# Induced attention and a squared-ReLU FFN on one core: a batch's product with w_in in four column strips, spread to all rows by way of DRAM

## The chip, the cores and the metric

The kernel runs on one core of a Trainium2 chip. A core has five engines, each with an instruction stream of its own and in order: TensorE (PE, with its weight loads shown as PEld), VectorE (DVE), ScalarE (ACT), GpSimd (POOL) and SyncE (SP), which here issues nearly all DMAs. The metric is the device time of one execution in microseconds: lower is better. Before the change it is 1634.57 us, the median of three runs (1631.74 to 1636.58).

## What is computed

Four batches of 12480 rows of 128 numbers go through two attentions and then an FFN. In the first attention 32 inducing rows ask and the batch's rows answer, which gives a small matrix h (32 x 128) for each batch; in the second the batch's rows ask and h answers. All of it is fp32.

```
def mab(q, kv):
    s = scale * (q @ kv.transpose(0, 2, 1))
    s = s - s.max(-1, keepdims=True)
    a = np.exp(s)
    a /= a.sum(-1, keepdims=True) + 1e-09
    return a @ kv
h = mab(I, x)              # I: 32 inducing rows; h: 32 x 128 a batch
out = mab(x, h)            # 12480 x 128 a batch
...
g = np.maximum(out @ w_in, 0.0)     # w_in: 128 x 2048
return g * g @ w_out                # w_out: 2048 x 128
```

## The kernel before, in words

**Tiles and stages.** A batch is cut into 13 units of 960 rows, 52 units in all, and a unit into two FFN blocks of 480 columns. `First` (L384) handles the first attention of a unit: load, transpose (by PE for the first batch, by VectorE's 32 x 32 transposes later), scores in four strips of 32 columns (L457), softmax parts, and a product that adds to h. `first_end` (L561) closes a batch: it joins the four partial h and brings them to SBUF as hT, which has 128 columns: each of the 32 rows of h stands there four times. `Second` (L651) makes the second attention's weights of a unit: scores in strips (L661, tile na), softmax by VectorE and ScalarE, a split into a high and a low part (tile sw, L707 and L710), and a trip through DRAM (tile far, L716) that brings the weights back as st, on all 128 rows (L721). `ffn_block` (L780) does the FFN.

**The product hw.** The second attention's a @ h and the FFN's product with w_in are joined: h @ w_in is made once per batch and the attention weights st are multiplied with it. In `first_end`, `wide(k)` (L619) multiplies hT with 512 of the 2048 columns of w_in for k = 0 to 3, into a PSUM bank of its own. All 128 rows come out, each row of h @ w_in four times. `part(k)` (L623, ScalarE) copies the 128 x 512 result, rounded to fp32r, into hw k; `rest(k)` (L627, VectorE) puts the remainder, the result less its rounded copy, into rows 64 to 127. So rows 0 to 63 hold the high parts and the others the low ones, and one fp32r product over 128 rows with st (whose rows hold high and low parts in turn) gives a nearly full fp32 product. There is one buffer for each hw k, so a new one can be written when the last readers of the old one, the h matmuls of quad k in the last block of the batch before, are done.

**The FFN block.** For each of the four quads j: four h matmuls (L802) with hw j and st, two relus (L810, ScalarE), one square (L820, ScalarE), the rounding to hi (L827 on VectorE, or a casting DMA issued by POOL, L825), the remainder lo (L831, VectorE), and twelve op matmuls (L847: hi with wo_hi, hi with wo_lo, lo with wo_hi). The h matmuls of a block run ahead of its op matmuls. A block ends with a transpose (L863) and four stores (L867).

**Weights.** At the start w_in and w_out, which arrive as pairs of 32-bit words, are turned into fp32 and, for w_out, split, by chains of VectorE, ScalarE and POOL steps (L280 to L309, L351, L368 to L373).

**The order of the work.** Every step is a task in a `Plan` (L45): an engine, a cost in ns, a due time, what it needs, which buffers it takes and reads. `Plan.run` (L81) is a list scheduler: on each engine it takes, of the tasks that could start now, the one with the earliest due time, and the order that comes out is the order of the program on each engine. A task of DMA has an issue time on SP, and lands later by 900 ns, its `moves` and 1000 ns (L149 to L151); buffers named in `IN_TURN` (L55), sw and xq among them, are taken in the order in which the tasks were added; a task that needs an SP task, and is on SP itself, may follow it directly in the plan (L93), and waits for the landing on the chip. The main loop (L902) runs over units with a `PERIOD` of 31000 ns; `PERIOD / 2` is a block. Before the change the four wides of a batch are due at 5/8 to 8/8 of the last unit of the batch before; in the start all four are due from `t_end + 2000` (L883) and the first scores of `Second` at `t_end + 2000` too (L886).

Of the kernel before, what the change touches and what calls it, by code (L numbers as in the profile page):

```python
# [11 lines left out]
F32 = mybir.dt.float32  # L12
F32R = mybir.dt.float32r
# [7 lines left out]
P = 128  # L21
TS = 120
NT = 8
UNIT = TS * NT
# [20 lines left out]
class Plan:  # L45
# [17 lines left out]
    def add(self, engine, ns, fn, due, needs=(), port=False, mode=None, takes=(), reads=(), late=None, moves=0.0, lag=0.0):  # L63

        if late is None:
            late = self.LATE["PE" if engine == "PE" else "other"] if due > self.begin else 0.0  # L70
        needs = [n for n in needs if n is not None]
        t = Task(engine.split("|"), ns, fn, due, needs, port, mode, takes, late, len(self.tasks), moves, lag)
        for b in list(takes) + list(reads):
            b.users.append(t)
        for b in takes:
            if b.tag in self.IN_TURN:
                b.turn = self.turns[b.tag] = self.turns.get(b.tag, -1) + 1
        self.tasks.append(t)
        return t
# [86 lines left out]
def induced_attention_then_squared_relu_ffn(  # L166
# [8 lines left out]
    nc = tc.nc  # L175
    B, N, C = x.shape
    M = inducing.shape[0]
    F = w_in.shape[1]
# [5 lines left out]
    NQ = NF // 4  # L184
    LANE, WIDE = UNIT // Q, 256
# [3 lines left out]
    PERIOD, START, T_MAIN, NARROW, STEP = 31000.0, 2500.0, 56000.0, -6000.0, 1700.0  # L189
    W_DUE = [12000.0 + 7500.0 * k for k in range(4)] + [40000.0 + 4000.0 * k for k in range(4)]  # L190
    W_AHEAD = 9000.0
    LAG, CAST_LAG, TWICE = 1500.0, 1500.0, (4, 8)

    ST = "ACT|DVE"
# [5 lines left out]
    xq_pool = ctx.enter_context(tc.tile_pool(name="xq", bufs=2))  # L200
    xt_pool = ctx.enter_context(tc.tile_pool(name="xt", bufs=NU + 2))
    hw_pool = ctx.enter_context(tc.tile_pool(name="hw", bufs=1))
    att = ctx.enter_context(tc.tile_pool(name="att", bufs=2))
    tiny = ctx.enter_context(tc.tile_pool(name="tiny", bufs=3))
    ps_h = ctx.enter_context(tc.tile_pool(name="ps_h", bufs=2, space=PSUM))
    ps_o = ctx.enter_context(tc.tile_pool(name="ps_o", bufs=2, space=PSUM))
    ps_m = ctx.enter_context(tc.tile_pool(name="ps_m", bufs=2, space=PSUM))
    far = ctx.enter_context(tc.tile_pool(name="far", bufs=2, space=bass.MemoryType.DRAM))
    plan = Plan(dict(xn=3, early=EB, xt=NU + 2, m=2, h=2, o=2, g=GB, hi=HB, lo=LB, st=2, sw=1, rows=1, xq=2, hw0=1, hw1=1, hw2=1, hw3=1, words=3, set=2), T_MAIN)

    def bank(name):
        return ps_m.tile([P, 512], F32, tag="m", name=name)
# [33 lines left out]
    add = plan.add  # L246
# [311 lines left out]
        t = add("PE", 520, mix, due, [f.et_done], mode="n", takes=[bank_h], reads=[f.bx])  # L558
        f.add_up(t, lambda: v["hp"], bank_h, due)

    def first_end(b, due, step, wide_due, wide_step):  # L561

        v = {}
        s = state[b]
# [44 lines left out]
            s["hT"] = att.tile([C, P], F32, tag="hT", name=f"hT_{b}")  # L609
            copy(tj, s["hT"], v["hp"][:C, :P])  # L610

        def wide(k):
            if b:
                v["wp", k] = bank(f"wp_{b}_{k}")
            elif k < 2:
                v["wp", k] = ps_h.tile([P, 2, 512], F32, tag="h", name=f"wp_{b}_{k}")[:, 0, :]
            else:
                v["wp", k] = ps_o.tile([P, 512], F32, tag="o", name=f"wp_{b}_{k}")
            nc.tensor.matmul(v["wp", k], s["hT"], w_in_sb[:, k * 512:(k + 1) * 512], start=True, stop=True)  # L619

        def part(k):
            s["hw", k] = hw_pool.tile([P, 512], F32R, tag=f"hw{k}", name=f"hw_{b}_{k}")
            nc.scalar.copy(s["hw", k], v["wp", k])  # L623

        def rest(k):
            lo = slice(2 * M, 4 * M)
            nc.vector.tensor_sub(s["hw", k][lo], v["wp", k][lo, :], s["hw", k][lo])  # L627

        bl, bz, bj = Buffer("m"), Buffer("m"), Buffer("m")
        t = add("DVE", 70, lanes, due, [last.shifted])  # L630
# [7 lines left out]
        t = add("DVE", 200, spread, due, [t])  # L638
        t = add("PE", 140, join, due + step, [t, last.summed], takes=[bj])
        tj = s["joined"] = add("ACT|DVE", (200, 200), joined, due + step, [t], reads=[bj])  # L640
        s["wide"] = []
        for k in range(F // 512):
            bw = Buffer("m" if b else "h" if k < 2 else "o")
            s["bhw", k] = Buffer(f"hw{k}")
            d = wide_due + k * wide_step
            t = add("PE", 870, lambda k=k: wide(k), d, [s["joined"], w_ins[k]], takes=[bw, s["bhw", k]])
            p = add("ACT", 650, lambda k=k: part(k), d, [t], reads=[bw, s["bhw", k]])
            s["wide"].append(add("DVE", 725, lambda k=k: rest(k), d, [p], reads=[bw, s["bhw", k]]))


    class Second:  # L651
# [228 lines left out]
        firsts[u] = First(0, u, 6000 + START * u, early=True)  # L880
        first_alone(firsts[u], 6000 + START * u)
    t_end = 6000 + START * NU + 2000
    first_end(0, t_end, 1000, t_end + 2000, 1000)  # L883
    t_main = T_MAIN
    seconds = {0: Second(0, 0)}
    narrow(seconds[0], None, None, t_end + 2000, 800)  # L886
    seconds[1] = Second(0, 1)
    narrow(seconds[1], None, None, t_end + 10000, 1700, seconds[0].split)
    opened = [add("POOL", 1, open_g, t_main - 2000, [firsts[NU - 1].summed])]
# [12 lines left out]
    for w, (b, u) in enumerate(units):  # L902
        t_u = t_main + w * PERIOD
        for k in range(2):
            ffn_block(b, u, k, seconds[w], t_u + k * PERIOD / 2, [] if w else opened)
        if w + 1 == len(units):
            break
        nxt = units[w + 1]
        if nxt[1] == 0:
            first_end(nxt[0], t_u - PERIOD / 2, 2000, t_u + PERIOD * 5 / 8, PERIOD / 8)  # L910
        before = seconds[w - 1].ready[1] if w else None
        if w:
            seconds[w + 1] = Second(*nxt)
        for m in range(1 + (w in TWICE)):
            g = firsts[done] if state.get("last") is not firsts[done] else None
            f = next_first(t_u + NARROW, seconds[0].ready[0])
            narrow(None if m or not w else seconds[w + 1], f, g, t_u + NARROW, STEP, before)
# [33 lines left out]
```

## Time and profile before

| | |
|---|---|
| median of 3 runs | 1634.57 us (1631.74 to 1636.58) |
| the profiled execution | 1636.69 us, span 1634.9 us, mean granted clock of TensorE 0.989 |
| PE busy | 1596.4 us |
| ScalarE busy | 1542.2 us |
| VectorE busy | 1461.1 us |
| wp matmuls (L619) | 32 instructions, two for each of the 16 products |
| hw copies (L623) and subtractions (L627) | 16 each |
| first FFN matmul h | at 77.38 us of the span |
| DMA | 311.00 MB, mean 190 GB/s |

The span runs from the first to the last instruction of the core. Busy time counts overlapping instructions of an engine once. An fp32 matmul appears as two instructions, an fp32r one as one; matmuls are pipelined, so that the distance between starts says more than the durations, which overlap. A row of the timeline gives start, busy time, engine, line, operation, output and inputs, count, and in brackets the idle time of the engine before it and what ended it. SPq rows are DMA issues by SP: the time is that of the issue, not of the transfer.

### The profile page before, as it was taken

What the parts mean: (1) busy time and instruction counts of PE and PEld (TensorE: products, weight loads), DVE (VectorE), ACT (ScalarE), POOL (GpSimd) and SP (SyncE); (2) the same over time, 40 slices, a digit from 0 to 9 for tenths busy, and PEclk for the clock granted to TensorE, in tenths of its full rate; (3) what the DMA queues carried; (4) which work ended last, traced back from release to release, by engine and by line L of the source; (5) the groups of instructions that cost most, each with busy time, mean ns of one, the idle gap of its engine ahead of it and who ended that gap; (6) DMA issues with size and microseconds to landing.
All of it is one profiled execution on the core that took longest, in us unless ns stands there. A gap on an engine that the chain in (4) does not pass through costs nothing.

```text
span 1634.9 us, 23534 instructions
## 1 busy us (share of the span) xinstructions
PE 1596.4 (98%) x8689; PEld 1325.2 (81%) x8689; DVE 1461.1 (89%) x1598; ACT 1542.2 (94%) x1566; POOL 124.0 (8%) x218
## 2 busy tenths in 40 slices
PE   7499999999999999999999999999999999999998
PEld 4278788888888888888887888888888888888887
DVE  5799989988999989999889999999888998989897
ACT  6399999999999999999998999999999999999996
POOL 1300000000000000000000000000000000000000
PEclk9699999999999999999999999999999999999999
DMA  9389988888777888788878878766555655565653
GB/s 230 71 123 202 217 217 199 212 211 210 188 207 199 209 211 203 211 207 210 217 182 202 209 207 203 211 190 190 164 181 160 190 184 172 181 199 169 192 172 95
DMA packets 474014, 311.00 MB, mean 190 GB/s; under 512 B 365212, under 2 KB 444668, under 8 KB 473900
## 3 DMA queue, kind: packets, MB, share of 16 engines
q1 hardware_dynamic: 445100, 112.89, 38.9%
q0 software_dynamic: 28800, 196.62, 33.9%
q8 instruction: 68, 1.11, 0.3%
q14 instruction: 46, 0.38, 0.1%
HBM read 74.50 MB, written 38.34 MB: 69 GB/s over the span
## 4 chain that ended last, share of the span: by engine, by line
PE 90%; DMA 3%; ACT 3%; DVE 2%; issue 1%; SPq 1%; DVEq 0%; ACTq 0%
PE op L847 63%; PE h L802 21%; PE na L661 2%; DMA xn<-in_x_dram 1%; ACT g L810 1%; ACT g L820 1%; PE wp L619 1%; PE na L457 1%; PE nb L508 1%; DVE lo L831 1%; DMA xq<-in_x_dram 1%; PE xtp L439 1%; PE ep L488 1%; DMA far<-sw 0%; PE sp L457 0%
## 5 line engine op out<-in xcount | busy, mean ns | idle before, releaser
L831 DVE TENSOR_TENSOR lo<-g,hi 128x1920 fp32r<-128x1920 f32 x416 | 883.6, 2145 | 28.5 <-PE op L847 23.1
L810 ACT ACTIVATE g<-h 128x960 f32<-128x960 f32 x832 | 781.2, 987 | 37.2 <-PE h L802 30.4
L820 ACT ACTIVATE g<-g 128x1920 f32<-128x1920 f32 x416 | 760.9, 1829 | 4.4
L802 PE MATMUL h<-st,hw 128*128 128x480 f32 x1664 | 504.6, 387 | 16.7 <-DMA st<-far 15.8
L847 PE MATMUL op<-hi,wo_lo 128*128 128x480 f32 x1664 | 472.0, 381 | 0.0
L847 PE MATMUL op<-hi,wo_hi 128*128 128x480 f32 x1664 | 442.3, 381 | 0.0
L847 PE MATMUL op<-lo,wo_hi 128*128 128x480 f32 x1664 | 435.0, 381 | 2.6 <-DVE lo L831 2.6
L802 PEld LDWEIGHTS h<-st,hw 128*128 128x128 f32 x1664 | 306.1, 189 | 78.6 <-DVE sw L710 15.8
L847 PEld LDWEIGHTS op<-lo,wo_hi 128*128 128x128 f32 x1664 | 309.9, 188 | 54.5 <-DVE lo L831 5.8
L847 PEld LDWEIGHTS op<-hi,wo_lo 128*128 128x128 f32 x1664 | 312.1, 188 | 50.9 <-issue 2.1
L847 PEld LDWEIGHTS op<-hi,wo_hi 128*128 128x128 f32 x1664 | 310.9, 188 | 49.8 <-issue 1.6
L827 DVE CAST hi<-g 128x1920 fp32r<-128x1920 f32 x216 | 248.4, 1152 | 37.5 <-PE op L847 26.6
L825 POOL DMA_DIRECT2D hi<-g x200 | 107.0, 535 | 1424.9 <-ACT g L810 279.3
L863 DVE STREAM_TRANSPOSE rows<-op 128x480 f32<-128x480 f32 x104 | 70.4, 677 | 51.2 <-PE op L847 49.5
L424 DVE STREAM_TRANSPOSE xt<-xq 128x960 f32<-128x960 f32 x39 | 45.6, 1170 | 8.6 <-DMA xq<-in_x_dram 6.0
L661 PEld LDWEIGHTS na<-xt,hT 128*32 128x32 f32 x520 | 19.9, 110 | 25.2 <-issue 19.4
L661 PE MATMUL na<-xt,hT 128*32 128x256 f32 (+2 forms) x520 | 34.9, 351 | 0.0
L685 ACT ACTIVATE d<-d 128x256 f32<-128x256 f32 x52 | 22.8, 439 | 7.0 <-DVE d L682 7.0
L689 DVE TENSOR_REDUCE z<-d 128x8 f32<-128x256 f32 x52 | 20.7, 398 | 8.4 <-ACT d L685 8.4
L508 PE MATMUL nb<-xn,et 120*32 120x128 f32 x624 | 25.7, 275 | 0.0
L457 PE MATMUL na<-xt,indT 128*32 128x240 f32 x312 | 24.8, 373 | 0.0
L703 DVE STREAM_TRANSPOSE a<-d 128x256 f32<-128x256 f32 x52 | 23.0, 443 | 1.3
(86 smaller groups left out, 529.6 us busy)
## 6 DMA issues: line engine op xcount, KB each, us to landing
hi<-g POOLq DMA_DIRECT2D x200, 960.0 KB, 4.5
xn<-in_x_dram SPq DMA_DIRECT2D x52, 480.0 KB, 6.3
st<-far SPq DMA_DIRECT2D x104, 240.0 KB, 4.3
out_dram<-rows SPq DMA_DIRECT2D x416, 60.0 KB, 3.5
xq<-in_x_dram SPq DMA_DIRECT2D x156, 120.0 KB, 5.3
far<-sw SPq DMA_DIRECT2D x52, 240.0 KB, 2.5
words_i<-in_moe_w_in_dram SPq DMA_DIRECT2D x4, 512.0 KB, 15.8
words_o<-in_moe_w_out_dram SPq DMA_DIRECT2D x4, 512.0 KB, 7.1
```

Of the source, the lines that this page charges most:

```text
L424: nc.vector.transpose(self.xt, v["xq"].rearrange("p g c -> p (g c)"))
L457: nc.tensor.matmul(to, indT, from_, start=True, stop=True)
L508: nc.tensor.matmul(where[q * M:(q + 1) * M, :], self.et[:, k, q * M:(q + 1) * M], self.xn[:, 2 * q + k, :], start=(k == 0), stop=(k == 1),)
L661: nc.tensor.matmul(where[q * M:(q + 1) * M, to:to + n], self.s["hT"][:, :2 * M].rearrange("c (m a) -> c m a", a=2)[:, :, 0], self.s["xt"][ ...
L802: nc.tensor.matmul(c["hp"][:, l, :BLK], s["hw", j][:, f % 4 * P:(f % 4 + 1) * P], s["st", u][:, k, :], start=True, stop=True,)
L810: nc.scalar.activation(v["g"][:, 2 * i:2 * i + 2, :], c["hp"][:, :, :BLK], AF.Relu)
L820: nc.scalar.activation(v["g"], v["g"], AF.Square)
L825: nc.gpsimd.dma_start(v["hi"], v["g"])
L827: nc.vector.tensor_copy(v["hi"], v["g"])
L831: nc.vector.tensor_sub(v["lo"], v["g"], v["hi"])
L847: nc.tensor.matmul(w["op"][:, :BLK], wo[:, 4 * j + l, :], v[name][:, l, :], start=len(done) == 1, stop=len(done) == 3 * NF,)
L863: nc.vector.transpose(w["rows"].rearrange("p g c -> p (g c)"), w["op"][:, :BLK])
```

## The change

`wide` becomes one task per batch: it multiplies the 32 distinct columns of hT (every second of the first 64) with each of the four parts of w_in, into the four strips of 32 rows of one PSUM bank. So the bank holds the 32 rows of h @ w_in once, 512 columns in each strip. `part(i)` and `rest(i)` then split the bank in two pieces of 256 columns, into a tile with a high and a low half: in the main loop this is the sw buffer that `Second` uses too (one buffer), in the start a room of the xq pool. `away(i)` sends the piece to DRAM, and `back_in(k)` brings strip k back to hw k with four DMAs of 32 rows of 512 numbers each, the high part to rows 0 to 63 (even rows and odd rows), the low part to rows 64 to 127. All copies wait for both aways. ScalarE and VectorE then work on 256 columns twice, where they had 512 columns four times. All of w_in has to be ready for the one task; before, each part of it alone.

The due times change as well: in the main loop the product is due 4000 ns before the last unit of the batch before begins, and the copies back from that unit's middle on, an eighth of the period apart. In the start the first scores of `Second` are due at `t_end + 500`, ahead of the product, which stays at `t_end + 2000`; the copies back are due from `t_end + 3000` on, 1000 apart.

```diff
+    WIDE_AT, BACK_AT = -4000.0, 0.0
...
-        def wide(k):
+        def wide():
+            v["wp"] = bank(f"wp_{b}")
+            thin = s["hT"][:, :2 * M].rearrange("c (m a) -> c m a", a=2)[:, :, 0]
+            for k in range(NQ):
+                nc.tensor.matmul(
+                    v["wp"][k * M:(k + 1) * M, :], thin, w_in_sb[:, k * 512:(k + 1) * 512], start=True, stop=True
+                )
+
+        def part(i):
             if b:
-                v["wp", k] = bank(f"wp_{b}_{k}")
-            elif k < 2:
-                v["wp", k] = ps_h.tile([P, 2, 512], F32, tag="h", name=f"wp_{b}_{k}")[:, 0, :]
+                v["hw", i] = att.tile([P, 2, WIDE], F32R, tag="sw", name=f"hwp_{b}_{i}", bufs=1)
             else:
-                v["wp", k] = ps_o.tile([P, 512], F32, tag="o", name=f"wp_{b}_{k}")
-            nc.tensor.matmul(v["wp", k], s["hT"], w_in_sb[:, k * 512:(k + 1) * 512], start=True, stop=True)
-
-        def part(k):
+                room = xq_pool.tile([P, UNIT // M, M], F32, tag="xq", name=f"hwp_{b}_{i}")
+                v["hw", i] = room.rearrange("p g c -> p (g c)")[:, :2 * WIDE].rearrange("p (j n) -> p j n", j=2).bitcast(F32R)
+            nc.scalar.copy(v["hw", i][:, 0, :], v["wp"][:, i * WIDE:(i + 1) * WIDE])
+
+        def rest(i):
+            nc.vector.tensor_sub(v["hw", i][:, 1, :], v["wp"][:, i * WIDE:(i + 1) * WIDE], v["hw", i][:, 0, :])
+
+        def away(i):
+            if i == 0:
+                v["far"] = far.tile([P, 2, 512], F32, tag="hwfar", name=f"hwfar_{b}", bufs=1)
+            nc.sync.dma_start(v["far"][:, :, i * WIDE:(i + 1) * WIDE], v["hw", i].bitcast(F32))
+
+        def back_in(k):
             s["hw", k] = hw_pool.tile([P, 512], F32R, tag=f"hw{k}", name=f"hw_{b}_{k}")
-            nc.scalar.copy(s["hw", k], v["wp", k])
-
-        def rest(k):
-            lo = slice(2 * M, 4 * M)
-            nc.vector.tensor_sub(s["hw", k][lo], v["wp", k][lo, :], s["hw", k][lo])
+            rows = s["hw", k].rearrange("(r a) n -> a r n", a=2).bitcast(F32)
+            for a in range(2):
+                for j in range(2):
+                    nc.sync.dma_start(rows[a, j * M:(j + 1) * M], v["far"][k * M:(k + 1) * M, j, :])
...
+        bw = Buffer("m")
+        t = add("PE", 950, wide, wide_due, [s["joined"]] + w_ins, takes=[bw])
+        far_done = []
+        for i in range(2):
+            bp = Buffer("sw" if b else "xq")
+            p = add("ACT", 420, lambda i=i: part(i), wide_due + 500, [t], takes=[bp], reads=[bw])
+            p = add("DVE", 400, lambda i=i: rest(i), wide_due + 1000, [p], reads=[bp, bw])
+            far_done.append(add("SP", 600, lambda i=i: away(i), wide_due + 2000, [p], reads=[bp], moves=1000))
         s["wide"] = []
-        for k in range(F // 512):
-            bw = Buffer("m" if b else "h" if k < 2 else "o")
-            s["bhw", k] = Buffer(f"hw{k}")
-            d = wide_due + k * wide_step
-            t = add("PE", 870, lambda k=k: wide(k), d, [s["joined"], w_ins[k]], takes=[bw, s["bhw", k]])
-            p = add("ACT", 650, lambda k=k: part(k), d, [t], reads=[bw, s["bhw", k]])
-            s["wide"].append(add("DVE", 725, lambda k=k: rest(k), d, [p], reads=[bw, s["bhw", k]]))
+        for k in range(NQ):
+            bh = s["bhw", k] = Buffer(f"hw{k}")
+            s["wide"].append(add("SP", 2400, lambda k=k: back_in(k), back_due + k * back_step, far_done, takes=[bh], moves=1000,
+                                 lag=LAG if b else 0.0))
...
-    first_end(0, t_end, 1000, t_end + 2000, 1000)
+    first_end(0, t_end, 1000, t_end + 2000, t_end + 3000, 1000)
...
-    narrow(seconds[0], None, None, t_end + 2000, 800)
+    narrow(seconds[0], None, None, t_end + 500, 800)
...
-            first_end(nxt[0], t_u - PERIOD / 2, 2000, t_u + PERIOD * 5 / 8, PERIOD / 8)
+            first_end(nxt[0], t_u - PERIOD / 2, 2000, t_u + WIDE_AT, t_u + PERIOD / 2 + BACK_AT, PERIOD / 8)
```

More of the change, by code (lines that the diff above doesn't have):

```diff
@@ L559, in mix_alone, with first_end @@
         f.add_up(t, lambda: v["hp"], bank_h, due)
-    def first_end(b, due, step, wide_due, wide_step):
+    def first_end(b, due, step, wide_due, back_due, back_step):
         v = {}
```

## The prediction

> **What bounds the kernel now.** I read the page first: busy times, then the chain that ended last.
>
> ```profile
> PE 1596.4 (98%) x8689; PEld 1325.2 (81%) x8689; DVE 1461.1 (89%) x1598; ACT 1542.2 (94%) x1566; POOL 124.0 (8%) x218
> ```
>
> ```profile
> PE 90%; DMA 3%; ACT 3%; DVE 2%; issue 1%; SPq 1%; DVEq 0%; ACTq 0%
> ```
>
> TensorE carries the chain, but ScalarE is close behind it. Averages hide stages, so I read the waits of PE next, and then the windows of one unit's length (29.9 us; columns: PE, PEld, DVE, ACT and POOL busy, granted clock, DMA share, GB/s).
>
> ```profile
> PE h L802 <- DMA st<-far: 15.8, 1, 15.8
> ```
>
> ```profile
> 436.20:466.10 29.90, 29.90 (x140) 24.17 (x142) 26.46 (x31) 29.50 (x32) 2.11 (x4) 1.00 0.78 180
> ```
>
> So there are two places. Once, before the first FFN block, PE stands still for 15.8 us until st arrives. After that it is busy without a gap: 29.90 of 29.90 us in the window that holds three of batch 1's four wp products. There, each us of work taken off PE is a us of the span as long as nothing else ends later, and the one to watch is ScalarE with 29.50 of 29.90.
>
> **Part 1: the products, in the three batch ends of the main loop.** The timeline of PE shows both a product as it is now and a score in strips (L661), which has the form that the change gives to the product.
>
> ```profile
> 462.21 1.02 PE L619 MATMUL wp<-w_in_sb,hT 128*128 128x512 f32 x2
> 462.67 0.99 PE L802 MATMUL h<-st,hw 128*128 128x480 f32 x2
> 463.50 0.60 PE L847 MATMUL op<-hi,wo_lo 128*128 128x480 f32 x2
> 463.93 1.02 PE L847 MATMUL op<-lo,wo_hi 128*128 128x480 f32 x4
> 464.79 0.60 PE L802 MATMUL h<-st,hw 128*128 128x480 f32 x2
> 465.23 0.60 PE L847 MATMUL op<-hi,wo_hi 128*128 128x480 f32 x2
> 465.76 0.63 PE L661 MATMUL na<-xt,hT 128*32 128x256 f32 x9
> 466.22 0.38 PE L457 MATMUL na<-xt,indT 128*32 128x240 f32 x3
> ...
> 467.21 0.71 PE L847 MATMUL op<-hi,wo_hi 128*128 128x480 f32 x2
> 467.76 0.60 PE L847 MATMUL op<-hi,wo_lo 128*128 128x480 f32 x2
> ```
>
> Ends are modelled, so I use starts. From 462.21 to 463.50 PE does one product wp (two instructions) and two h; 1.29 us. Two FFN matmuls take 0.43 (the pair at 463.50 is followed at 463.93). So one product takes 0.86, and the four of a batch 3.44 us.
>
> The scores of a second unit are strips side by side: from 465.76 to 466.22 four strips of up to 256 columns and a stub of 16 pass in 0.46 us. One after another, at the rate of wp (0.86 for 512 columns), they would have taken 4 x 0.43 = 1.72. So strips do overlap here. For 512 columns I double it: 0.92. Around such a group there is a price for going over to strips and back: 465.23 plus 0.43 is 465.66, so 0.10 goes before the group, and the pair after it takes 0.55 (467.21 to 467.76) where 0.43 is normal, 0.12 more. Product in strips: 0.92 + 0.22 = 1.14. PE saves 3.44 - 1.14 = 2.30 per batch, 6.9 us over three batches. Ends for this term: without the price of going over, 2.52 x 3 = 7.6; if strips overlapped in pairs only (2 x 0.86 + 0.22 = 1.94), 1.50 x 3 = 4.5. I take 6.9, since the row that shows strips is this kernel's own.
>
> The Trainium skill, "TensorE: Matmul & The Clock Gate", section "Measured speedup vs the span model", gives 2.38x for three column strips of 512. By that rate four products would cost an estimated 3.44 / 2.38 = 1.45 us of strips and the term would be 3 x (3.44 - 1.67) = 5.3; the 0.46 us above speaks for nearly full overlap, and the sum stays with the row.
>
> **Part 2: the split, in the loop.** What is removed and what takes its place:
>
> ```profile
> L623 ACT CAST hw<-wp x16: 567/586/597, 56.4 to 1249.9; 128x512 fp32r<-128x512 f32 x16
> ```
>
> ```profile
> L627 DVE TENSOR_TENSOR hw<-wp,hw x16: 694/695/696, 57.0 to 1253.3; 64x512 fp32r<-64x512 f32 x16
> ```
>
> ```profile
> L250 ACT COPY et<-ep 120x256 f32<-120x256 f32 x3 | 1.2, 388 | 0.0
> ```
>
> ```profile
> L675 DVE STREAM_TRANSPOSE d<-na 128x256 f32<-128x256 f32 x3 | 1.3, 436 | 0.0
> ```
>
> ScalarE gives up 4 x 0.586 = 2.34 and gets two copies of 256 columns from PSUM, 2 x 0.388 (L250's row) = 0.78: 1.57 less per batch. VectorE gives up 4 x 0.695 = 2.78 and gets two of 0.436 (L675's row): 1.91 less. Both lie beside PE and are counted at nothing. If PE were not the bound there, ScalarE's 1.57 would be the gain (a rival below).
>
> The split now holds one psum bank for both parts, and the second part reuses the one sw buffer. So part(1), on ScalarE, waits until the first away has landed. Behind it on ScalarE stand the relus and squares; for the relus PE waits, which has only two h banks.
>
> ```profile
> L716 SPq DMA_DIRECT2D far<-sw x52: 552/552/1260, 70.0 to 1573.0; - x52
> ```
>
> ```profile
> DMA to landing us min/median/max: 2.5/2.5/7.4
> ```
>
> The kernel's plan knows this wait: it allows about 0.6 + 0.9 + 1.0 + 1.0 and 0.2 of margin, 3.7 us from the away's start, and lets other ScalarE work go first. A transfer of this size lands in 2.5 at the median, 7.4 at most. So the wait costs from 0 to 3.7 us per batch; I take 0, as the median is the nearest value.
>
> **Part 3: the copies, in the loop.** SP gets 18 more issues per batch: two aways, and sixteen copies back of 64 KB each.
>
> ```profile
> L867 SPq DMA_DIRECT2D out_dram<-rows x416: 315/497/2941, 104.6 to 1631.9; - x139
> ```
>
> ```profile
> L420 SPq DMA_DIRECT2D xq<-in_x_dram x156: 322/672/3862, 73.9 to 1072.5; - x156
> ```
>
> ```profile
> st<-far SPq DMA_DIRECT2D x104, 240.0 KB, 4.3
> ```
>
> ```profile
> 455.69 3.35 SPq L867 DMA_DIRECT2D out_dram<-rows  x4
> 467.36 0.34 SPq L400 DMA_DIRECT2D xn<-in_x_dram  x1
> 468.57 8.26 SPq L420 DMA_DIRECT2D xq<-in_x_dram  x4
> ```
>
> The nearest row is the store, 60 KB over 32 rows in runs of four: 0.497 each. Sixteen take 8.0 us, four of them 2.0. hw of quad k is free when its last reader in the last block is done and is needed one block, 15 us (half of 29.9), later. Four issues and a landing (4.3, as st's) are 6.3 us: 8.7 to spare, so it costs nothing. Each copy waits at the head of SP for PE's readers; stores, loads and st queue behind it. SP has a gap of 8.3 us here (459.04 to 467.36), and no engine needs those transfers at once. Were this cover gone, each us by which hw is late would be one of PE.
>
> **Part 4: the start.** Here the change moves the order: the first scores now come ahead of the product on PE, and the copies of hw come ahead of st on SP.
>
> ```profile
> 53.91 0.27 ACT L250 COPY hT<-htp 128x128 f32<-128x128 f32 x1 [3.79 <-PE htp L606]
> ```
>
> ```profile
> 54.32 2.05 PE L619 MATMUL wp<-w_in_sb,hT 128*128 128x512 f32 x2 [0.45 <-ACT hT L250]
> 56.30 1.11 PE L661 MATMUL na<-xt,hT 128*32 128x256 f32 x10
> ...
> 77.38 1.14 PE L802 MATMUL h<-st,hw 128*128 128x480 f32 x2 [15.76 <-DMA st<-far]
> ```
>
> ```profile
> 58.23 0.42 DVE L679 TENSOR_REDUCE mx<-d 128x8 f32<-128x256 f32 x1
> ...
> 61.68 0.69 DVE L627 TENSOR_TENSOR hw<-wp,hw 64x512 fp32r<-64x512 f32 x1 [0.16 <-ACT hw L623]
> 62.41 0.43 DVE L682 TENSOR_TENSOR d<-d,mx 128x256 f32<-128x256 f32 x1
> ```
>
> ```profile
> 70.04 0.64 SPq L716 DMA_DIRECT2D far<-sw  x1
> 72.59 1.27 SPq L721 DMA_DIRECT2D st<-far  x2
> ```
>
> ```profile
> 54.30:61.70 7.40, 7.30 (x28) 2.84 (x28) 2.97 (x6) 3.38 (x6) 2.53 (x2) 0.68 0.01 2
> ```
>
> Two paths then meet at st. The softmax path: na starts at 54.3 instead of 56.30, 2.0 earlier. Now, 3.8 us pass between the maximum (ends 58.65) and the subtraction (62.41), with three rests in them; the change leaves two short ones, and I credit 2.5 of the 3.8. So sw is ready at 70.04 - 4.5 = 65.5.
>
> The hw path: na is done at 55.4; the strips take what one product takes there, 2.05 (the granted clock in this stretch was 0.68), so 57.5; copy 0.39, subtraction 0.44, the second pair beside them, two aways of 0.55 each: the second starts at about 59.3 and lands 2.5 later, with 0.2 of handing over at 62.0. By the due times in the code SP then issues the copies of hw0 to hw2 (12 x 0.497 = 6.0, to 68.0), st's away (0.64, to 68.6), the copies of hw3 (2.0, to 70.6), and only then st. st's away has landed by 70.5, so st is issued at 70.6, where it was 72.59: 2.0 earlier, and first h with it at 75.4. PE stays idle for it all the same; what is late next is SP's queue, no longer the softmax. Ends: at 0.32 a copy (the least in both rows) hw2 is out at 65.8, st's away lands at 68.3, the gain is 4.3; at 0.672 (the median of xq) st goes at 73.4, a loss of 0.8. I take 0.497, the row nearest in size and rows. The loads of x behind st move with it.
>
> **The sum.** The profiled execution took 1636.69 us (span 1634.9): less 6.9 and 2.0 is 1627.8. It lies 2.1 above the median of the runs, 1634.57; against that the forecast is 1634.57 - 8.9 = 1625.7.
>
> **Rivals.** *The copies go one at a time.* For: the four xq at 468.57 take 8.26 us, 2.07 each. Against: their median is 0.672, the stores' 0.497. At 2.07 the sixteen and st's away would take 33.8 us from 62.0, st would leave at 95.8 and the first h come 23 us late: 1634.6 - 6.9 + 23.2 = 1651, slower. It decides from where the start loses more than the loop's 6.9: st at 79.5, so (79.5 - 62.0 - 0.64) / 16 = 1.05 us a copy. The Trainium skill, "DMA: Bandwidth & Descriptors", section "Rules for kernel authors", says that transfers to disjoint partitions serialize and that one of 128 partitions should be used; with its fit of 2.0 us plus bytes an estimated 16 x 2.15 = 34 us would pass, the same end. The medians above are against it. Chance 0.08.
>
> *ScalarE waits for the first part's landing* (part 2). For: a landing of 7.4 has been seen, and ScalarE has 0.4 us to spare in the window. Against: median 2.5, and the plan's allowance of 3.7. At 2 us a batch it takes 6 back, 1631.7, which is within 0.3%; at the full 3.7 it is 1636.8, still within. Chance 0.12.
>
> *ScalarE is the bound at the batch ends.* Then a batch gains 1.57, not 2.30: 4.7 + 2.0, 1627.9. For: 29.50 of 29.90. Against: PE shows no gap there. Chance 0.20.
>
> *The strips don't overlap*, so that the change doesn't do what it says: 4 x 0.86 + 0.22 costs 0.2 more per batch and the start's gain goes with the later product: about 1635. The strips of L661 speak against it. Chance 0.03.
>
> **How the numbers follow.** The forecast has 0.55; 0.02 is left for what I don't see. A measurement of this kernel can tell about 0.3%, 4.9 us, from no change. Faster by more than that (below 1629.7) are the forecast and ScalarE as bound, 0.75, less 0.01 for their edges: 0.74. Within it are the waiting ScalarE, the strips and the rest: 0.17. Slower: 0.09, nearly all from the copies. The range takes the ends of the two terms (7.6 + 4.3 gives 1622.7, 4.5 less 0.8 gives 1630.9), 1.7 below for the spread of runs, and above reaches into the case of the waiting ScalarE: 1621 to 1633.
>
> **What would show it.** In the profile after: wp (now strips) with a spacing of some 1.1 us between its neighbours in the loop; the first h at about 75.4, st issued after the last copy of hw; copies on SP at about 0.5 apiece in the start; PE still 29.9 of 29.9 in the batch ends. Wrong if PE waits for hw or st at a batch end, if ScalarE shows an idle stretch before the second part, or if the copies are over 1 us apart.

## The result, and the profile after

The changed kernel takes 1650.97 us at the median of six runs, the kernel before 1634.68 in the same comparison: a ratio of 1.0097, with a 95% interval from 1.0083 to 1.0112. That is 16 us slower, where 9 us faster was forecast. One of the six executions took 2125.95 us at a granted clock of 0.689; the comparison leaves it out, and the profile read here is of another execution of the changed kernel, of 1648.56 us (span 1646.8, mean granted clock 0.984), beside which the kernel before took 1634.24.

The busy times and the chain that ended last, on the page of the changed kernel:

```profile
PE 1591.8 (97%) x8689; PEld 1323.9 (80%) x8689; DVE 1450.1 (88%) x1590; ACT 1534.8 (93%) x1558; POOL 123.5 (8%) x218
```

```profile
PE 90%; DVE 3%; DMA 3%; ACT 2%; SPq 1%; issue 1%; DVEq 0%; ACTq 0%; POOLq 0%
```

These two lines tell almost nothing: PE is busy 4.6 us less, ScalarE and VectorE are relieved as meant, and the chain looks as it did. What is new stands in the waits of PE:

```profile
PE h L822 <- DMA st<-far: 19.4, 1, 19.4
PE h L822 <- DMA hw<-hwfar: 12.1, 3, 6.2
```

By its name the new wait is for hw; which transfer each of these rests hung on is read further down. The windows of the three batch ends (columns as in the prediction: length, PE, PEld, DVE, ACT, POOL, granted clock, DMA share, GB/s):

```profile
436.20:466.10 29.90, 28.80 (x158) 23.48 (x157) 26.96 (x29) 28.71 (x30) 2.11 (x4) 1.00 0.80 206
466.10:496.00 29.90, 22.90 (x123) 18.51 (x122) 17.39 (x22) 19.34 (x21) 1.58 (x3) 0.89 0.92 210
854.80:884.70 29.90, 24.82 (x138) 20.32 (x128) 20.75 (x29) 19.49 (x22) 1.59 (x3) 0.89 0.88 194
1243.50:1273.40 29.90, 27.86 (x122) 23.61 (x121) 24.63 (x24) 25.84 (x23) 2.11 (x4) 0.94 0.73 208
```

The second and the third of them in the kernel before (the prediction shows the first; the last is as full, 29.90):

```profile
466.10:496.00 29.90, 29.90 (x192) 24.64 (x185) 28.16 (x33) 28.59 (x30) 1.59 (x3) 1.00 0.85 209
854.80:884.70 29.90, 29.36 (x188) 23.52 (x187) 26.96 (x32) 25.19 (x28) 1.59 (x3) 1.00 0.81 190
```

PE stands still for 1.10 + 7.00 + 5.08 + 2.04 = 15.2 us in these four windows, where it stood for 0.5 before. And the three windows with a long rest in them were granted 0.89, 0.89 and 0.94 of the clock. If all of their busy time ran at that mean, it would have cost (22.90 + 24.82) x 0.11 + 27.86 x 0.06 = 6.9 us, an estimate. The stretches with the lower clock give the same: from 481.3 to 488.1, from 870.4 to 877.2 and from 1259.5 to 1262.9 us it was granted at 0.50, and PE was busy for 4.53, 5.80 and 3.40 us of them, half of which is 6.9. So 14.7 more of idle time, some 6.9 of slow clock, less the 6.9 forecast for the strips: some 14.7, against 11.9 between the two profiled spans, 14.3 between the two executions of that comparison and 16 between the medians.

The Trainium skill, "TensorE: Matmul & The Clock Gate", section "HAM oscillation — how this bites in real kernels", says that PE-idle gaps over about 3.4 us throttle the clock again. The gaps of 6.2 and 5.08 us agree with it; the longest recorded gap of the last window is 2.0 us and it fell to 0.94 all the same, for which that rule has no reason.

Who held hw back is seen on SP, at the end of batch 1 (start, time of issue, line, tiles, count):

```profile
450.10 2.41 SPq L642 DMA_DIRECT2D hw<-hwfar  x4
452.61 4.07 SPq L887 DMA_DIRECT2D out_dram<-rows  x4
456.77 0.56 SPq L736 DMA_DIRECT2D far<-sw  x1
459.94 1.28 SPq L741 DMA_DIRECT2D st<-far  x2
461.31 6.93 SPq L642 DMA_DIRECT2D hw<-hwfar  x8
468.29 0.59 SPq L401 DMA_DIRECT2D xn<-in_x_dram  x1
468.97 5.49 SPq L421 DMA_DIRECT2D xq<-in_x_dram  x4
474.56 5.81 SPq L642 DMA_DIRECT2D hw<-hwfar  x4
```

```profile
476.32 1.03 PE L867 MATMUL op<-lo,wo_hi 128*128 128x480 f32 x4
483.57 1.94 PE L822 MATMUL h<-st,hw 128*128 128x480 f32 x4 [6.22 <-DMA hw<-hwfar]
```

The rest of SP of 8.3 us, on which the prediction leaned, is gone: from 450.10 to 480.37 SP has no gap of note but one, of 2.6 us, in which st waits at its head for far to land. The sixteen copies take 2.41 + 6.93 + 5.81 = 15.15 us of it, 0.95 each. The copy of hw 3 stands last: st, eight other copies and five loads of x go first. It lands at about 483.4 and PE, whose FFN is out of work at 477.35, has waited for 6.2 us. Before that, at 468.88, PE had waited 0.78 us for the copies of hw 1.

Batch 2 shows a second way in which the change delays PE. Here is the end of VectorE's split into sw, the first weights of the new batch, before and after:

```profile
838.61 0.43 DVE L710 TENSOR_TENSOR sw<-a,sw 128x256 fp32r<-128x256 f32 x1
```

```profile
854.22 0.42 DVE L730 TENSOR_TENSOR sw<-a,sw 128x256 fp32r<-128x256 f32 x1
```

The split ends 15.6 us later. Its buffer is the one in which part(0) and then part(1) of hw lay, each until its away had landed (the two aways were issued from 839.58 to 847.58). Then SP comes on top: stores and four copies are ahead of far, which goes at 858.78, and st leaves at 863.85. PE's rest of 5.08 us ends at 871.40 with the first four h of the new batch, which need hw 0 and st. The view names hw as what it waited for, but that hw 0 had been sent from 849.57 on, and st was the late one, by its time from issue to landing:

```profile
L741 SPq DMA_DIRECT2D st<-far x2: 613/713/813, 863.8 to 864.5; - x2
DMA to landing us min/median/max: 6.3/6.5/6.7
```

The second of the two, issued at 864.5, took the 6.7 and landed at 871.3, just ahead of PE's start. The rest of 2.04 us at the end of batch 3 is of the same kind: the view names a square of ScalarE, but the second half of st, issued at 1251.4, landed after 6.8 us at 1258.2, and PE went on at 1258.32. A rest of 0.63 us, at batch 1's end, ended like this too, at 465.03, with st landed at 464.9. Of the 15.2 us, then, 7.0 are waits for hw, all at batch 1's end, and 7.75 are waits for st, at all three.

### The profile page after: what moved, and what is told of

It is laid out like the page before. It is cut to its first block, busy times and chain, and to the rows that moved or that the text cites. A ratio compares the mean times of both kernels' runs of the same rounds, so it can differ in the third digit from the quotient of the medians.

```text
span 2124.2 us, 23623 instructions
## 1 busy us (share of the span) xinstructions
PE 2089.6 (98%) x8689; PEld 1437.5 (68%) x8689; DVE 1467.2 (69%) x1590; ACT 1578.7 (74%) x1558; POOL 122.6 (6%) x218
## 4 chain that ended last, share of the span: by engine, by line
PE 98%; DVE 1%; DMA 0%; ACT 0%; SPq 0%; issue 0%; ACTq 0%
PE op L867 68%; PE h L822 23%; PE na L681 2%; PE nb L509 1%; PE na L458 1%; PE ep L489 1%; PE xtp L440 1%; PE hp L509 0%; PE sp L458 0%; DMA xn<-in_x_dram 0%; PE wp L617 0%; DMA xq<-in_x_dram 0%; ACT g L830 0%; SPq L642 0%; DVE a_o L300 0%
## 5 line engine op out<-in xcount | busy, mean ns | idle before, releaser
L822 PE MATMUL h<-st,hw 128*128 128x480 f32 x1664 | 627.5, 469 | 20.4 <-DMA st<-far 19.5
L867 PE MATMUL op<-hi,wo_lo 128*128 128x480 f32 x1664 | 603.0, 467 | 0.0
L867 PE MATMUL op<-hi,wo_hi 128*128 128x480 f32 x1664 | 575.7, 468 | 0.0
L867 PE MATMUL op<-lo,wo_hi 128*128 128x480 f32 x1664 | 561.2, 468 | 0.0
L822 PEld LDWEIGHTS h<-st,hw 128*128 128x128 f32 x1664 | 338.0, 205 | 165.3 <-issue 40.2
L867 PEld LDWEIGHTS op<-hi,wo_lo 128*128 128x128 f32 x1664 | 339.1, 204 | 140.4 <-issue 17.2
L867 PEld LDWEIGHTS op<-lo,wo_hi 128*128 128x128 f32 x1664 | 336.4, 203 | 140.4 <-issue 19.1
L867 PEld LDWEIGHTS op<-hi,wo_hi 128*128 128x128 f32 x1664 | 336.5, 203 | 139.8 <-issue 19.6
L251 ACT COPY et<-ep 120x256 f32<-120x256 f32 x52 | 19.3, 372 | 38.0 <-PE ep L489 38.0
L509 PEld LDWEIGHTS nb<-xn,et 120*32 120x32 f32 x624 | 20.6, 114 | 13.8 <-issue 8.8
```

Of the source, the lines that this page charges most:

```text
L509: nc.tensor.matmul(where[q * M:(q + 1) * M, :], self.et[:, k, q * M:(q + 1) * M], self.xn[:, 2 * q + k, :], start=(k == 0), stop=(k == 1),)
L822: nc.tensor.matmul(c["hp"][:, l, :BLK], s["hw", j][:, f % 4 * P:(f % 4 + 1) * P], s["st", u][:, k, :], start=True, stop=True,)
L867: nc.tensor.matmul(w["op"][:, :BLK], wo[:, 4 * j + l, :], v[name][:, l, :], start=len(done) == 1, stop=len(done) == 3 * NF,)
```

## The experiments

**Theory 1**: SP issues in order, and with 18 more issues at each batch end it is full, so that hw, or st behind hw, comes late. **Theory 2**: the two parts hold the sw buffer through two landings, so the new batch's first sw, and with it st, comes late. **Theory 3**: not the number of issues but the bytes, 1 MB back in per batch, slow the transfers down. In the diffs, lines are those of the changed kernel.

**a0_after.** The changed kernel without an edit, for a profile.

> The changed kernel itself, unaltered, for an undisturbed trace. First theory: the 16 us that it lost lie at the three batch ends of the main loop, since the first h started at the same time as before; then PE shows idle stretches there of some 5 us each, ended by the landing of a copy of hw (theory 1) or by ScalarE, which stood waiting for the first part's landing (theory 2). Rival: the loss is spread over all units (theory 3), by DMA traffic or by another order of the steps, and then no stretch of PE stands out. About 1650 us in all three cases.

It took 1648.56 us, and its profile is the one read above.

**e1_nocopy.** No copies in the loop:

```diff
+            if b:
+                s["wide"].append(add("POOL", 1, lambda k=k: s.update({("hw", k): state[0]["hw", k]}), back_due + k * back_step, far_done))
+                continue
```

> The product in strips, its split and the aways stay, but in the three batch ends of the main loop nothing is copied back (batches 1 to 3 use the hw of batch 0, so that part of the result is left out). Theory 1 (SP's queue, in order, is the bound at a batch end: what hangs on it, hw or st, comes late): without the sixteen issues the waits of PE go, and what is left is the saving of the strips, 1634.7 less 6.9, so 1627 to 1629. Theory 2 (the parts hold the sw buffer and the PSUM bank, so the first st of the new batch is late): those waits stay, some 7 of the 13 us that PE now stands still or runs slow at the second and third batch end, 1637 or more. Theory 3 (the traffic of the copies): like theory 1.

1635.24 us, ratio 1.0009 (0.9989 to 1.0028): the copies cost 16 us, the whole loss. But the saving didn't appear either. The profiled execution, at 1647.13 the slowest of ten and the only one with a trace, shows why that can be:

```profile
PE h L826 <- DMA st<-far: 28.9, 3, 19.5
```

Twice, for 9.4 us in all, PE waited for st at a batch end, with no copy in the queue. That speaks for theory 2.

**e2_pool_queue.** The loop's copies are issued by POOL:

```diff
-                    nc.sync.dma_start(rows[a, j * M:(j + 1) * M], v["far"][k * M:(k + 1) * M, j, :])
+                    (nc.gpsimd if b else nc.sync).dma_start(rows[a, j * M:(j + 1) * M], v["far"][k * M:(k + 1) * M, j, :])
```

> All copies stay, those of the main loop are issued by POOL instead of SP; POOL issues only the casts there. Theory 1: SP is free of them, 1627 to 1632. Theory 2: no gain at the second and third batch end, 1637 or more. Theory 3 (the same bytes on the same DMA engines): no gain at all, 1648 to 1651.

1646.83 us (1639.33 to 1650.69), ratio 1.0065 (1.0040 to 1.0089). No wait for hw is left, but another took its place:

```profile
PE h L822 <- DMA st<-far: 23.7, 2, 19.5
PE op L867 <- DVE lo L851: 10.9, 7, 8.2
```

The 4.2 us that the first line has beyond the start's 19.5 are at batch 2's end, as theory 2 has it. The longest wait for lo, 8.2 us, ends at 527.30, over 60 us after POOL issued the last copy of that batch end (462.56 to 464.58). VectorE, which makes lo, stood in front of it for the rows buffer of the block before:

```profile
524.52 0.68 DVE L883 STREAM_TRANSPOSE rows<-op 128x480 f32<-128x480 f32 x1 [7.71 <-DMA out_dram<-rows]
```

The stores of that block left SP only from 517.37 to 521.71, behind loads of x (6.32 us for four), far (3.43 us for one issue) and st. So with the copies on another engine it is still the queue of SP that runs late; what made its issues slow there was not tried apart. The Trainium skill, "DMA: Bandwidth & Descriptors", section "Rules for kernel authors", says that spreading DMAs over the issuing engines only saves the sequencer's issue time; the gain over the changed kernel, 4 us between medians whose intervals overlap, agrees.

**e3_half_issues.** Scratch DRAM holds each piece twice, row beside row, so that a copy back fills 64 rows:

```diff
-            nc.sync.dma_start(v["far"][:, :, i * WIDE:(i + 1) * WIDE], v["hw", i].bitcast(F32))
+            for a in range(2):
+                nc.sync.dma_start(
+                    v["far"][:, :, a, i * WIDE:(i + 1) * WIDE].rearrange("j p n -> p j n"), v["hw", i].bitcast(F32)
+                )
...
-            for a in range(2):
-                for j in range(2):
-                    nc.sync.dma_start(rows[a, j * M:(j + 1) * M], v["far"][k * M:(k + 1) * M, j, :])
+            for j in range(2):
+                nc.sync.dma_start(
+                    s["hw", k][2 * j * M:2 * (j + 1) * M].bitcast(F32), v["far"][j, k * M:(k + 1) * M].rearrange("m a n -> (m a) n")
+                )
```

> The parts go to DRAM twice, row by row, and come back in two copies of 64 rows for each hw instead of four of 32: per batch 4 aways and 8 copies instead of 2 and 16, the bytes back as before, the bytes away doubled. Theory 1: SP is relieved of 6 of 18 issues, some 4 us per batch end, of the 5 to 8 us by which hw or st is late: 1633 to 1642. Theory 2: unchanged or worse, 1650. Theory 3: more bytes, so worse, 1650 or more.

1641.85 us, ratio 1.0033 (1.0012 to 1.0054): 9 us better with twelve issues in place of 18, the same bytes back and twice the bytes away. By the names of the view the wait for hw hardly fell (11.2 us, from 12.1). By the landings the gain is st's: of the 7.75 us for which PE waited for st at the batch ends 1.3 are left, while the waits for hw grew from 7.0 to 9.9. The rest in the start went from 19.4 to 16.2. Theory 3 alone would have had no gain.

**e4_own_buffer and e5_own_buffer_nocopy.** The parts get a buffer of their own; room for it comes from a single tile d in `Second` and from hT, which keeps 64 columns. The second kernel has no copies either, as e1.

```diff
-                v["hw", i] = att.tile([P, 2, WIDE], F32R, tag="sw", name=f"hwp_{b}_{i}", bufs=1)
+                v["hw", i] = att.tile([P, 2, WIDE], F32R, tag="hwp", name=f"hwp_{b}_{i}", bufs=1)
...
-            bp = Buffer("sw" if b else "xq")
+            bp = Buffer("hwp" if b else "xq")
...
-                v["d"] = tile_of("d")
+                v["d"] = tile_of("d", 1)
```

> The changed kernel, but the parts of hw get a buffer of their own instead of the sw buffer of the second attention (room for it: one tile d instead of two, and hT with its 64 used columns alone). After the run without the copies, which came out at 1635, two causes are held: theory 1, SP's queue with the sixteen copies (about 16 us of the loss), and theory 2, the sw buffer, which the first unit of a new batch gets only after two transfers have landed, so that its st is late (about 7 us, what was missing there from 1628). Theory 2 alone right: 1634 or less for this kernel. Both: 1640 to 1645, as the copies stay. Theory 1 alone: 1649 to 1651, as now.

> The own buffer, and no copies back in the main loop (batches 1 to 3 use the hw of batch 0: that part of the result is left out). Theories 1 and 2 together: no wait is left at the batch ends and only the saving of the strips stands, 1627 to 1629. If it stays at 1633 to 1636, as with the sw buffer, theory 2 falls and the saving on PE was mis-sized.

1653.16 us (ratio 1.0111, 1.0096 to 1.0126) and 1634.87 (0.9997, 0.9988 to 1.0007). Read by themselves these times say that theory 2 is worth nothing. The windows say otherwise. Here are two of e5, the second at batch 1's end:

```profile
137.00:197.00 60.00, 52.20 (x296) 42.11 (x289) 50.35 (x65) 49.85 (x56) 3.80 (x7) 0.94 1.05 211
466.10:496.00 29.90, 29.90 (x153) 25.37 (x144) 27.18 (x30) 29.09 (x30) 2.11 (x4) 1.00 0.80 212
```

The batch end is full, but far from any batch end PE now stands for 7.8 of 60 us, where the kernel before stood for 1.9 (58.12 busy): the single d moved the order of the work there. The edit had a side effect as large as what it was to measure, so both kernels were made anew, as e8 and e9.

**e6_own_half_issues and e7_own_half_loads.** e4 with e3's halved issues; and that with the x loads of a batch's second unit put behind the last copy of hw:

```diff
-            f = next_first(t_u + NARROW, seconds[0].ready[0])
+            f = next_first(t_u + NARROW, state[b]["wide"][-1] if b and not u else seconds[0].ready[0])
```

> The own buffer, and twelve issues per batch end instead of eighteen (parts sent away twice, back in two copies of 64 rows for each hw). Theories 1 and 2: with fewer issues hw comes earlier, 1629 to 1638, and below the run with the own buffer alone. If the bytes count and not the issues: at or above that run.

> As the run before, and the loads of x that the plan puts between the copies of hw of a batch end have to come after the last of them. Theory 1 (order on SP): PE no longer waits for hw, 1627 to 1632. If the waits move to the loads, na or st (another step of the same queue): no better than the run before.

1641.86 us (ratio 1.0042, 1.0018 to 1.0066), with the stretch at 137 us still in it, and 1675.55 (1.0266, 1.0238 to 1.0294), a miss. The loads did leave hw's way, and then what needs x was late. Of PE's waits in e7:

```profile
PE op L871 <- DVE lo L855: 13.8, 4, 5.9
...
PE h L826 <- DMA hw<-hwfar: 2.0, 1, 2.0
```

The wait for hw is down to 2.0 us (5.7 in e6), while lo costs 13.8 (0.8 in e6). "No engine needs those transfers at once", as the prediction put it of the loads, is true for a few us only.

**e8_own_no_side and e9_own_no_side_nocopy.** The parts' own buffer, with room made where nothing else is touched: hT and join keep the 64 columns that the strips read, and the inducing rows lie in an xn tile. e9 has no copies in the loop.

```diff
-    ind_sb = const.tile([M, C], F32, name="ind_sb")
+    ind_sb = xn_pool.tile([TS, NT, C], F32, tag="xn", name="ind_sb")[:M, 0, :]
...
-            v["join"] = att.tile([P, P], F32, tag="join", name=f"join_{b}", bufs=1)
+            v["join"] = att.tile([P, 2 * M], F32, tag="join", name=f"join_{b}", bufs=1)
...
-            s["hT"] = att.tile([C, P], F32, tag="hT", name=f"hT_{b}")
+            s["hT"] = att.tile([C, 2 * M], F32, tag="hT", name=f"hT_{b}")
```

> The own buffer for the parts once more, now without touching d (the two runs before with an own buffer and one d had a new wait of some 7 us at 170 us of the span, before any batch end, which hides the comparison): room is made by hT and join with their 64 used columns, and the inducing rows in a tile of x. The order of all steps up to the first batch end is that of the changed kernel. Theories 1 and 2 together: 1641 to 1647, the copies' part of the loss is left. Theory 1 alone: 1649 to 1651.

> The same with no copies back in the main loop (batches 1 to 3 use the hw of batch 0: that part of the result is left out). Theories 1 and 2 together: no wait at the batch ends and none new at 170 us, so the saving of the strips is seen, 1627 to 1629. If it stays at 1634 to 1636, the saving on PE was mis-sized.

1643.04 us (ratio 1.0058, 1.0040 to 1.0075): the buffer alone gives 8 of the 16 us back. PE's waits in e8 show how:

```profile
PE h L822 <- DMA st<-far: 19.5, 1, 19.5
PE h L822 <- DMA hw<-hwfar: 9.1, 3, 4.0
```

The one wait for st is the start's; at the batch ends none is left, and what PE mainly waits for there is hw, 3.20 us at batch 1's end and 1.80 and 4.05 at batch 2's. That is theory 2 shown, and theory 1 beside it.

e9 took 1630.31 (0.9969, 0.9953 to 0.9986): with the copies gone as well, the change is faster, by 4.3 us at the medians. The two costs overlap, since a late st and a late hw delay the same PE: without the copies 15.7 us come back, with the buffer 7.9, with both 20.7. This is the ceiling for the loop; two windows of e9:

```profile
137.00:197.00 60.00, 56.09 (x310) 46.02 (x302) 53.14 (x65) 54.45 (x59) 4.38 (x8) 0.97 1.03 215
466.10:496.00 29.90, 29.90 (x167) 25.05 (x166) 26.99 (x29) 29.36 (x30) 2.12 (x4) 1.00 0.84 207
```

**e10_thin_copies and e12_own_no_side_thin.** As many copies with an eighth of the bytes, first in the changed kernel, then in e8:

```diff
-                    nc.sync.dma_start(rows[a, j * M:(j + 1) * M], v["far"][k * M:(k + 1) * M, j, :])
+                    nc.sync.dma_start(rows[a, j * M:(j + 1) * M, :w], v["far"][k * M:(k + 1) * M, j, :w])
```

Here w is 64 in the loop and 512 in the start.

> The changed kernel, sw buffer and all, with its sixteen copies per batch end, but each brings 64 of 512 columns (in batches 1 to 3 the other columns of hw stay those of batch 0: that part of the result is left out). Same issues, same order, an eighth of the bytes. Theory 1, issues and order on SP: 1645 to 1651, nearly unchanged. Theory 3, bytes on the DMA engines: as without copies, 1634 to 1637.

> The parts have a buffer of their own (and no side edit of the d tile), and in the three batch ends of the loop the sixteen copies back stay sixteen but carry 64 of the 512 columns each; the rest of hw stays that of batch 0 (this leaves out most of hw of batches 1 to 3). With sixteen whole copies this kernel took 1643.0 us, with no copies 1630.3. Theory 1 (the number of issues and their place in SP's order hold the batch end up): near 1640, above 1637. Rival (the 1.05 MB a batch hold it up, the number of issues does not): near 1631, below 1634. Between 1634 and 1637 both hold a share.

1643.73 us (ratio 1.0060, 1.0045 to 1.0075) and 1635.36 (1.0000, 0.9984 to 1.0015). With the sw buffer, thin copies cost 8.5 us (over e1's 1635.24) where whole ones cost 15.7; with a buffer of their own 5.0 (over e9) where whole ones cost 12.7. So theory 3 doesn't have it all: some 40% (5.0 of 12.7) to 54% (8.5 of 15.7) of the cost stays with an eighth of the bytes.

The rest is not shown to be the bytes', for the edit has a side effect: the 64 columns lie in the first part, so a thin copy doesn't wait for the second away. At batch 2's end of e12 the second away was issued at 847.76 and landed 6.0 us later, and the first copy left at 848.43; in e8, the second away, issued at 848.85, took 6.2, and the first copy left at 855.07, right behind its landing. That is the batch end at which e8's PE waited 1.80 and 4.05 us for hw, and e12's not at all. At batch 1's end the second away had landed before the copies began in both; SP there, first e8, then e12:

```profile
463.88 3.96 SPq L642 DMA_DIRECT2D hw<-hwfar  x4
467.93 6.44 SPq L421 DMA_DIRECT2D xq<-in_x_dram  x4
474.47 3.99 SPq L642 DMA_DIRECT2D hw<-hwfar  x4
```

```profile
464.35 3.58 SPq L643 DMA_DIRECT2D hw<-hwfar  x4
468.02 4.18 SPq L421 DMA_DIRECT2D xq<-in_x_dram  x4
472.30 3.48 SPq L643 DMA_DIRECT2D hw<-hwfar  x4
```

The thin copies take SP nearly as long as the whole ones: 13.8 us for the sixteen of this batch end, against 14.2. It is the loads between them that are issued faster, 4.18 in place of 6.44 us, so that hw 3 leaves 2.2 us earlier. PE got nothing of it here: its wait for hw 3 is 3.35 us in e12, 3.20 in e8.

**e11_own_no_side_half and e13_own_no_side_half_again.** e8 with e3's four aways and eight copies of 64 rows: the same kernel in two comparisons.

> The own buffer without the side wait, and twelve issues per batch end instead of eighteen. Theories 1 and 2: between the run with all copies and the one with none, 1630 to 1637; this is the version that could beat both kernels. If bytes count: no better than the run with all copies.

> The parts' own buffer with four aways and eight copies of 64 rows, the same kernel as in the run before with this edit (1631.1 us, ratio 0.999 with an interval from 0.9972 to 1.0007). What is open is whether it is faster than the kernel before. If it keeps the strips' saving at the ceiling (1630.3 without any copies) it is 1630 to 1632 and its interval lies below 1; if the waits for hw (3.5 us in the profiled execution) vary from run to run, the interval takes in 1 again.

1631.11 us (ratio 0.9990, 0.9972 to 1.0007) and 1630.53 (0.9971, 0.9957 to 0.9985). The second clears 1 and the first takes it in; both medians lie 3.5 to 4.1 us under the kernel before. This version keeps the strips and beats the changed kernel by 20 us, and the kernel before by a little. Of its waits, and its window at batch 1's end, which was granted the full clock, in e13:

```profile
PE h L825 <- DMA st<-far: 16.1, 1, 16.1
PE h L825 <- DMA hw<-hwfar: 2.3, 2, 2.0
```

```profile
466.10:496.00 29.90, 27.86 (x157) 22.95 (x156) 25.04 (x28) 27.18 (x30) 2.11 (x4) 1.00 0.93 228
```

Part of its gain is the start's (below, 3.4 us), which e9 does not have; so in the loop the eight copies still cost an estimated 3.6 us, where sixteen cost 12.7.

## Why the prediction was wrong, point by point

**Part 1 held.** PE's rows of the changed kernel around the strips:

```profile
433.99 0.59 PE L867 MATMUL op<-hi,wo_hi 128*128 128x480 f32 x2
434.51 1.07 PE L617 MATMUL wp<-w_in_sb,hT 128*32 128x512 f32 x8
435.50 0.43 PE L489 MATMUL ep<-ident,e 128*120 128x128 f32 x2
435.69 0.68 PE L867 MATMUL op<-hi,wo_hi 128*128 128x480 f32 x2
436.21 0.59 PE L867 MATMUL op<-hi,wo_lo 128*128 128x480 f32 x2
```

The strips take 0.99 us, and the pairs ahead and behind 0.52 each where 0.43 is normal: 0.99 + 0.18 = 1.17 against 1.14 forecast. The product shrank as computed, by 2.3 us a batch. At the ceiling (e9) the runs gave 4.3 of the 6.9 us, an interval of 2.3 to 7.7 by its ratio; its profile has 2.0 us more idle time than before in the window at 137 us, and 1.2 more at 436 us (28.67 busy, with a wait for a relu behind the second part), which would make up the difference.

**Part 2 looked at the wrong waiter.** It priced the reuse of the sw buffer as ScalarE's wait for the first away, and counted 0. That wait was there and small: 1.10 us before the second part at 444.59 of batch 1, and PE stood 0.46 for the relu behind it. What the step left out is who else needs that buffer: the new batch's sw, and with it st, for which PE stood 7.75 us at the batch ends. An own buffer gave back 8 us (1650.97 to 1643.04), half of the loss.

**Part 3 is the step that failed**: "Four issues and a landing (4.3, as st's) are 6.3 us: 8.7 to spare, so it costs nothing." It priced the copies of one quad as if they were issued the moment that their buffer came free. SP takes its list in order, and the copy of hw 3 had st, eight other copies and five loads ahead of it. The size was off as well: 0.95 us per copy at this batch end, not 0.497, which makes 15.2 us of SP's time for sixteen, where 8.0 were put into a gap of 8.3. What it said of the loss of this cover ("each us by which hw is late would be one of PE") came true: 7.0 us of PE's waiting for hw at batch 1's end, and 9.05 at two batch ends in e8, where st no longer came late, with the clock's loss beside it. "No engine needs those transfers at once" was wrong of st, which stood behind four copies at batch 2's end and which PE waited for.

**Part 4's size was wrong by its whole gain.** From the copy of hT to the first h of the FFN it took 77.38 - 53.91 = 23.47 us before and 73.80 - 50.36 = 23.44 after (hT itself came earlier in this execution). The order was as foreseen; SP in the start of the changed kernel:

```profile
58.12 7.52 SPq L642 DMA_DIRECT2D hw<-hwfar  x12
65.73 0.55 SPq L736 DMA_DIRECT2D far<-sw  x1
66.33 2.53 SPq L642 DMA_DIRECT2D hw<-hwfar  x4
68.95 1.27 SPq L741 DMA_DIRECT2D st<-far  x2
```

Sixteen copies took 10.05 us, 0.63 each, not 8.0: those 2.0 us are the forecast's gain. The upper bound that the text had, 0.672, was the better price. With eight copies of 64 rows (e13) the same distance is 73.86 - 53.81 = 20.05, 3.4 us less: it was SP's queue that the start hung on.

**The rivals.** The rival of copies one at a time gave 1651, the time that came, by a mechanism that did not: the copies' median issue is 0.592 us, below its point of 1.05, and the start lost nothing. The Trainium skill's rule beside it, that transfers to disjoint partitions serialize and one of 128 should be used, is borne out in its advice (halving the copies gained 9 to 12.5 us). The price that the prediction worked out beside it is not: the sixteen copies of the start took 10.05 us and not 34. The Trainium skill gives the fit that this price came from for DMAs issued by GpSimd (same page, section "Anatomy of one DMA — SWDGE (gpsimd) path"), and these are issued by SP.

Strips that don't overlap are refuted by the strips' rows. ScalarE as the bound (a gain of 4.7 in the loop) is not refuted by e9's time, whose interval of 2.3 to 7.7 takes in 4.7 as well as 6.9; against it speaks e9's window at 466 us, where PE is busy for all of 29.90. ScalarE's wait for the first part's landing came at batch 1's end alone; PE lost 0.46 us by it in the changed kernel and 0.5 to 1.7 in e8 to e13, less than that rival's 2 to 3.7 a batch. What happened was named only as a sign, "wrong if PE waits for hw or st at a batch end", and had no chance of its own.

**Open.** Why the single d of e4 to e7 moves the stretch at 137 us, and whether the bytes of the copies cost anything beside their number, was not tried apart: the thin copies lost a wait along with their bytes, and their rows are 256 bytes long where they were 2 KB.

## What to carry to other kernels

A queue that issues in order is a resource like an engine: before new DMAs are called free, write down all that it has to issue in that stretch, in its order, with the waits at its head, and read off when the last new one leaves. Ask of every buffer that is borrowed for a trip through DRAM who needs it next, for it is held until the landing, not until the issue. And a saving on the bound engine is real only while its inputs still come in time: here 6.9 us of work saved, spread over three places, set off 15 us of waiting at the same three. Last, where a view names what ended a wait, look whether that transfer had landed long before: two of the three rests of over 2 us here bore the wrong name.

## What the runs showed of the hardware

The issue time of a DMA on SP is not a property of the DMA alone: 64 KB copies were issued in 0.45 us at the least, 0.592 at the median and 2.80 at most, and 0.95 on average where SP was full; copies of 8 KB kept the same median:

```profile
L642 SPq DMA_DIRECT2D hw<-hwfar x64: 450/592/2801, 58.1 to 1264.3; - x64
```

```profile
L643 SPq DMA_DIRECT2D hw<-hwfar x64: 442/592/1704, 59.9 to 1245.7; - x64
```

The first line is of the changed kernel, the second of e12, where 48 of the 64 copies carry an eighth. And the 8 KB copies did not land sooner:

```profile
hw<-hwfar SPq DMA_DIRECT2D x48, 64.0 KB, 3.4
hw<-hwfar SPq DMA_DIRECT2D x48, 8.0 KB, 3.7
```

The first line is of the loop of e8, the second of that of e12, which has the same buffers: 3.4 us at the median for 64 KB, 3.7 for 8 KB.
